# Three eighths of one streamed V unit held on chip, an eighth of it in the scores' PSUM bank; raw left rows by slot; streamed units at new places

## The chip, the cores and the metric

One core of one Trainium2 chip. The metric is the device time of one execution in microseconds (us), the median of several.

## The reference

Two branches on the layer-normed rows of x (2048 rows of 1024), added to x:

```python
x = A_x
xn = _layernorm(x, axis=-1)
return x + _A_ref(xn, ...) + _B_ref(xn, ...)      # B: gelu(xn @ w1 + b1) @ w2 + b2, F = 3584
...
for s in range(64):                                # A: 64 segments of 32 rows, 8 memory rows ahead of each
    h = concatenate([mem, xs])
    q, k, v = h @ Wq, h @ Wk, h @ Wv               # each 1024 x 4096: 32 heads of 128
    p = softmax(mask(q k^T / sqrt(128)))
    o = (p v) @ Wo                                 # 4096 x 1024
    mem = o[:8]                                    # goes into the next segment
    outs.append(o[8:])
```

The memory rows make the segments a chain. Wq, Wk, Wv and Wo are 8 MB each in bf16, 32 MB together, and are multiplied anew in every segment; they don't fit on chip.

## The kernel before

The program first computes branch B (to about 400 us of the profile), and then runs the loop over the 64 segments.

**Units.** The four weights are cut into 64 units of 128x2048 bf16 (512 KB): (w, i, u) is row block i and half u of the columns for K, Q and V; an O unit is two heads. `ORDER` takes them pass by pass: K0, Q0, K1, Q1, V0, V1 of eight units each, then 16 O units. 47 units are resident in SBUF. The other 17 are streamed: `PLACED` holds four strings of passes, one for each type of segment (s mod 4), where "S" is a place for a streamed unit and "." for a resident one. The first string also says which units are streamed.

**Streams.** Six SBUF slots take the streamed units in turn. `unit_done` follows the last product of a streamed unit and calls `start_stream`, which starts the next unit into the slot just freed: a DMA on SP's queue from a packed DRAM copy (`Wc_...`), 128 rows of 4096 B. So a start runs six streamed units ahead of its use. Two of the 17 units are not fetched: `IN_PSUM` and `IN_BANKS` are kept in two PSUM banks each, and `copy_bits` (L274, DVE) copies them into the slot; `late_by` starts them `LATER` = 4 places later.

**Left rows.** The last 8 of a segment's 32 rows don't depend on the memory. Those of four segments (a group) are multiplied as one set of 32 rows, `hL`, as extra "left" products beside the 24 + 8 rows of the segment: K0 and K1 in type 0, V0 in type 1, Q0 and V1 in type 2, Q1 in type 3; O in type 3 takes them with a wider accumulator. `hL` is renewed for the next group in three pieces: slots 0 and 1 after K1 of type 0, slot 2 after Q0 of type 2, slot 3 after Q1 of type 3 (`renew_left`, by DVE in the first seven segments, then by POOL). The raw rows lie in a tile of their own, `left_rows_in` (128x256), loaded once a group (L297) before O of type 3. `VL[u]` (128x512) holds the left values by slot, 128 columns each; `by_slot` writes all of VL[0] at the start of type 2 and all of VL[1] at the start of type 3, and a segment reads the columns of its own slot.

**A segment.** Six passes of products (L831), with the attention of the first half of the heads placed into K1, Q1 and V1, that of the second half into V1 and O. The tables `SCORES_0`, `SUMS_0`, `ATTEND`, `VALUES_0`, `SUMS_1` and `VALUES_1` say after which unit of a pass each step comes, by type. Scores, sums and the memory's transpose (`put_mem`) use one PSUM bank, `mixed`:

```python
mixed = banks.tile([P, 512], F32, name="mixed", ...)   # 0:224 scores, 0:320 sums, 224:288 put_mem, 468:512 masks
```

O's products (L1068) end in `fold` (types 0 to 2), whose result goes through `put_mem` into the next segment's rows. While DVE does that, PE computes up to six left products of the next segment's pass ahead (`lead_products`). Every engine runs its instructions in the order in which they are written here.

Of the kernel before, what the change touches and what calls it, by code (L numbers as in the profile page):

```python
# [10 lines left out]
BF16 = mybir.dt.bfloat16  # L11
U32 = mybir.dt.uint32
# [5 lines left out]
P = 128  # L18
S = 2048
# [5 lines left out]
SEG = 32  # L25
MEM = 8
NSEG = S // SEG
KT = DM // P
# [9 lines left out]
NX = 24  # L38
NL = SEG - NX
GRP = 4  # L40
# [14 lines left out]
MEM_AT = 20  # L55
EARLY_SEGS = 7
LEAD_FIRST = 4
SCORES_0 = (6, 6, 6, 6)
SUMS_0 = (4, 4, 4, 4)
ATTEND = (0, 0, 1, 0)  # L60
VALUES_0 = ((4, 4), (4, 4), (3, 5), (4, 4))
SUMS_1 = (6, 6, 5, 7)
VALUES_1 = (5, 5, 5, 5)
LATER = 4
LAG = 3
STREAM_BUFS = 6
# [7 lines left out]
def pass_order():  # L74
# [12 lines left out]

ORDER = pass_order()
PLACED = (
    "..SS...." ".S..S..." "S....S.." "S......S" "S......." "S.S...S." "...SS..." "S....S.S",  # L90
    ".S.S...." "S....S.." ".S.S...." "....S..S" "......S." "SS...S.." "....S.S." "S....SS.",
    "..SS...." ".S..S..." "S...S..." "....S.S." "..S....." "...S.S.S" "...S..S." "S....SS.",
    "...SS..." ".S..S..." "..S..S.." ".SS....." "..S....." "S...S..S" "...S..S." "S....S.S",
)
IS_STREAMED = {unit: PLACED[0][n] == "S" for n, unit in enumerate(ORDER)}
assert all(placed.count("S") == STREAMED for placed in PLACED)
# [13 lines left out]
RESIDENT = [unit for unit in ORDER if not IS_STREAMED[unit]]  # L110

IN_PSUM = [unit for unit in ORDER if IS_STREAMED[unit]][3]
STREAMED_O = [unit for unit in ORDER[48:] if IS_STREAMED[unit]]

IN_BANKS = STREAMED_O[AT_BANKS]
# [5 lines left out]
def kernel(  # L121
# [16 lines left out]
    nc = tc.nc  # L138
# [38 lines left out]
    slabs = ctx.enter_context(tc.tile_pool(name="slabs", bufs=1))  # L177
    consts = ctx.enter_context(tc.tile_pool(name="consts", bufs=1))
    hrp = ctx.enter_context(tc.tile_pool(name="hrp", bufs=1))
    left_rows_in = hrp.tile([P, 256], BF16, name="left_rows_in")  # L180
    hL = hrp.tile([P, 256], BF16, name="hrL").rearrange("p (k t) -> p k t", k=KT)
    ctx.enter_context(tc.manual_schedule())

# [52 lines left out]
    for k in range(7):  # L236
# [4 lines left out]
    res_tiles = {}  # L241


    copies = {
        unit: dram.tile([P, 2048], BF16, name="Wc_" + "_".join(map(str, unit)))[:, :]
        for unit in reversed(ORDER) if IS_STREAMED[unit] and unit not in KEPT
    }

    def fetch(t, unit):
        w, i, u = unit  # L250
        if w == "O":
            h = 4 * i + 2 * u
            nc.sync.dma_start(out=t.rearrange("p (h d) -> p h d", d=DM), in_=Wo_v[:, h:h + 2, :])
        else:
            nc.sync.dma_start(out=t, in_=W_v[w][:, i, 2048 * u:2048 * u + 2048])

    def fetch_resident(*places):
        for place in places:
# [13 lines left out]
    def copy_bits(out, in_):  # L272

        nc.vector.tensor_single_scalar(out=out, in_=in_, scalar=0, op=ALU.bitwise_or)  # L274

    def start_stream(slot):
        if not starts:
            return
        n = starts.popleft()
        unit, t = streams[n], slab(slot)  # L280
        if unit in kept_in:
            for c0, bank in kept_in[unit]:
                copy_bits(t[:, c0:c0 + 1024].bitcast(U32), bank.bitcast(U32))
        elif unit in copies:
            nc.sync.dma_start(out=t[:, :], in_=copies[unit])
        else:
            fetch(t[:, :], unit)
        stream_tiles[n], slot_of[n] = t, slot

    nxt, kept_in = {}, {}  # L290

    def load_x_rows(s, eng=nc.sync):
        eng.dma_start(out=homes[s % 2], in_=rows_d[s, :, :])
        nxt["hT"] = homes[s % 2].rearrange("p (k t) -> p k t", k=KT)

    def load_left_rows(g, out, eng=nc.sync):
        eng.dma_start(out=out, in_=rowsL_d[g, :, :])  # L297

    def renew_left(rows, s0, s1, eng):

        eng.tensor_copy(
            out=hL.rearrange("p k (t s) -> p k t s", s=GRP)[:, :, :, s0:s1],
            in_=rows.rearrange("p (k s t) -> p k t s", k=KT, s=GRP)[:, :, :, s0:s1],
        )

    sp = ctx.enter_context(tc.tile_pool(name="sp", bufs=1))
# [50 lines left out]
    with tc.tile_pool(name="ma", bufs=2) as ma:  # L357
# [112 lines left out]
                    )  # L470

        def keep_xT(tg, xnT):
            xl = [t[:, 0:512].rearrange("p (g k i t) -> p g k i t", g=2, k=KT, i=GRP) for t in ko_flat]
            for half in range(2):
                nc.sync.dma_start(
                    out=rows_d[16 * tg:16 * tg + 16, :, 128 * half:128 * half + 128].rearrange("s p c -> p s c"),
                    in_=xnT[half].rearrange("p s k t -> p s (k t)"),
                )
                for g in range(4):
                    nc.gpsimd.tensor_copy(  # L480
                        out=xl[g // 2][:, g % 2, 4 * half:4 * half + 4, :, :],
                        in_=xnT[half][:, 4 * g:4 * g + 4, :, NX:SEG].rearrange("p i k t -> p k i t"),
                    )
            for k in range(2):
                nc.sync.dma_start(
                    out=rowsL_d[4 * tg + 2 * k:4 * tg + 2 * k + 2, :, :].rearrange("g p c -> p g c"),
                    in_=xl[k][:, :, :, :, :].rearrange("p g k i t -> p g (k i t)"),
                )

        def keep_R(ttg, rsb):  # L490
# [92 lines left out]
        for tg in range(4):  # L583
            last = tg == 3
            if last:

                load_x_rows(0)
                load_left_rows(0, pd_main[:, 0:256])
                load_left_rows(1, left_rows_in[:, :])
# [146 lines left out]
    with tc.tile_pool(name="late", bufs=1) as late:  # L736
# [60 lines left out]

        hT = nxt["hT"]
        VL = [late.tile([P, 512], BF16, name=f"VL{u}") for u in range(2)]
        led = {}  # L800

        for s in range(NSEG):
# [16 lines left out]
            mover = nc.vector if s < EARLY_SEGS else nc.gpsimd  # L819
            st = {}  # L820

            def product(w, i, t, lhs, acc, seq, left=False):
                for j in range(4):
                    o, m = acc[32 * j:32 * j + 32, :], t[:, 512 * j:512 * j + 512]
                    if w != "V":
                        o = o.rearrange("p (h e) -> p h e", e=32)
                        m = t.rearrange("p (h q e) -> p q h e", q=4, e=32)[:, j, :, :]
                    elif left:
                        o = o.rearrange("p (q c e) -> p q c e", q=4, e=32)
                        m = m.rearrange("p (c q e) -> p q c e", q=4, e=32)  # L830
                    nc.tensor.matmul(  # L831
                        o,
                        lhsT=lhs[:, i, :],
                        rhs=m,
                        start=(i == seq[0]),
                        stop=(i == seq[-1]),
                        tile_position=(0, 32 * j),
                    )

            def lead_products(n):  # L840

                w, u, psL, ahead, order = led["next"]
                for _ in range(n):
                    if led["made"] < len(ahead):
                        i = ahead[led["made"]]
                        product(w, i, res_tiles[w, i, u], hL, psL, order, True)
                        led["made"] += 1

            def half_pass(w, u, left, at, left_done=None):
# [13 lines left out]
                for n in range(KT + lag):  # L863
                    if n < KT:
                        tiles[now[n]] = unit_tile((w, now[n], u))
                        product(w, now[n], tiles[now[n]], hT, ps, now)
                    if n < lag:
                        continue
                    i = now[n - lag]
                    t = tiles.pop(i)  # L870
                    if left and i not in ahead:
                        product(w, i, t, hL, psL, order, True)
# [216 lines left out]
            if first:  # L1089
                keep(IN_BANKS, 1024, d_oL[:, 0:DM], 2)  # L1090
                keep(IN_BANKS, 0, kq[:, 0:DM], 3)
                copy_bits(mixed[:, 468:512].bitcast(U32), mask.bitcast(U32))
            psK, psKL = half_pass(
                "K", 0, left_k[0], {0: [lambda: by_slot(i4 - 2, qL_flat[i4 - 2])]} if i4 >= 2 else {},
                lambda ps: turn_kL(ps, 0),
# [8 lines left out]
            psQ, psQL = half_pass("Q", 0, left_q[0], {} if left_q[0] else {1: [lambda: q_left(0)]}, first_queries)  # L1104
            turn_q(psQ)
            if i4 == 2 and more:
                renew_left(left_rows_in, 2, 3, mover)
            psK1, psK1L = half_pass("K", 1, left_k[1], {SCORES_0[i4]: [lambda: scores(0)]})
            if i4 == 0 and not first and more:
                renew_left(left_rows_in, 0, 2, mover)  # L1110
            exps(0)
            st["kT", 1] = nat_home
            rows_out(psK1, nat_home, nc.scalar.copy)
# [8 lines left out]
                q_left(1)  # L1122
            turn_q(psQ1)
            if i4 == 3 and more:
                renew_left(left_rows_in, 3, 4, mover)
            if not final and not first:
                load_x_rows(s + 1, loads)

# [26 lines left out]
                staged(1)(psV1L)  # L1155
            if first:
                by_slot(1, hr_home)
                renew_left(left_rows_in, 0, 2, mover)
                load_x_rows(s + 1, loads)
            loads.dma_start(out=homes[s % 2], in_=res_d[s + 1, :, :])  # L1160
            if i4 == 3 and g + 2 < NGRP:
                load_left_rows(g + 2, left_rows_in[:, :])
            at = {VALUES_1[i4]: [lambda: values(1, (0, 1))]}
            psX = new_acc()
            for n, unit in enumerate(O_UNITS):
# [5 lines left out]
                unit_done(unit)  # L1171
                for fn in at.get(n, ()):
                    fn()
                if n == 6 and left_o:
                    st["resL"] = pd_main[:, 0:256]
                    loads.dma_start(
                        out=st["resL"], in_=resL_d[g, :, :]
                    )
# [97 lines left out]
```

## Time and profile before

| | us |
|---|---|
| median of 3 runs | 1772.6 |
| lowest, highest | 1770.92, 1780.19 |
| profiled execution | 1783.28 |
| its span, first to last instruction | 1781.5 |

| engine | busy in the span |
|---|---|
| PE (products) | 1694.8 us, 95% |
| DVE | 1019.5 us, 57% |
| ACT | 696.5 us, 39% |
| POOL | 287.2 us, 16% |

The profile shows the core's engines (PE, its weight loads PEld, DVE, ACT, POOL, and SP, which only issues DMAs here) and 16 DMA engines, which all queues share. "SPq" is SP's queue of DMA issues. In a row of instructions, "x48" is a count, and the brackets hold the engine's idle time before it and who ended it. A row of waits has the total in us, the number of waits and the longest. "DMA share" is the mean busy share of the 16 DMA engines. The granted clock of PE was 0.996.

### The profile page before, as it was taken

To read this page: it belongs to the slowest core of one execution; us is meant where nothing else is said; L and a number is where in the kernel's file an instruction comes from. 1 tells how busy PE (TensorE), PEld (TensorE's weight loads), DVE (VectorE), ACT (ScalarE), POOL (GpSimd) and SP (SyncE) were. 2 spreads that over 40 slices of the span, in tenths; PEclk is the share of its full clock that TensorE was granted. 3 is DMA by queue.
4 is the path that set the end of the run, shared out by engine and by line. 5 is a ranking of instruction groups with operands and counts; after the bars stand their busy time and mean duration, and the time that the engine had idled before them with its cause. 6 is when DMAs were issued, how large, how long until landed. Compare 5 with 4: busy or idle time off the path is not lost.

```text
span 1781.5 us, 65947 instructions
## 1 busy us (share of the span) xinstructions
PE 1694.8 (95%) x28354; PEld 838.9 (47%) x28374; DVE 1019.5 (57%) x2592; ACT 696.5 (39%) x1743; POOL 287.2 (16%) x575
## 2 busy tenths in 40 slices
PE   9999999998998999999999999999999999999998
PEld 5444444444444444444444444444444444444444
DVE  7657483825555565655655555555565656565564
ACT  6334251602333444433344333443333444343333
POOL 0000002403120211111211111121111121111120
PEclk9999999999999999999999999999999999999999
DMA  9455312779999999999999999999999999999997
GB/s 283 141 171 167 98 36 66 272 270 322 387 379 364 384 387 383 399 377 395 384 384 387 376 378 384 394 369 388 382 400 377 398 378 393 387 401 372 393 385 295
DMA packets 232072, 591.85 MB, mean 332 GB/s; under 512 B 57523, under 2 KB 88051, under 8 KB 231780
## 3 DMA queue, kind: packets, MB, share of 16 engines
q1 hardware_dynamic: 199680, 568.05, 84.7%
q0 software_dynamic: 15680, 14.35, 2.5%
q10 hardware_dynamic: 16420, 5.25, 1.2%
q8 instruction: 222, 3.64, 0.8%
q14 instruction: 70, 0.57, 0.1%
HBM read 571.50 MB, written 26.74 MB: 336 GB/s over the span
## 4 chain that ended last, share of the span: by engine, by line
PE 41%; DMA 20%; DVE 5%; ACT 3%; issue 1%; DVEq 0%; SPq 0%; ACTq 0%
PE acc L831 27%; PE acc L1068 11%; DMA u<-Wc_O 8%; DMA u<-Wc_Q 5%; DMA u<-Wc_V 3%; DMA u<-Wc_K 2%; PE acc L1018 1%; DVE kq L919 1%; DMA hr_home<-res_d 1%; ACT mixed L991 1%; ACT qL L885 1%; PE mixed L944 1%; DVE pd_main L999 1%; PE mixed L328 1%; PE acc L1024 0%
## 5 line engine op out<-in xcount | busy, mean ns | idle before, releaser
L831 PE MATMUL acc<-u,hr_home 128*32 128x512 bf16 x11520 | 758.1, 381 | 37.1 <-DMA u<-Wc_V 19.7
L831 PEld LDWEIGHTS <-hr_home 128*32 128x32 bf16 x12288 | 333.0, 97 | 336.7 <-issue 58.4
L831 PE MATMUL acc<-u,hrL 128*32 128x512 bf16 x3008 | 258.8, 381 | 0.5 <-issue 0.5
L532 PE MATMUL ps<-u 128*128 128x512 bf16 (+1 forms) x992 | 195.0, 359 | 0.0
L885 ACT CAST d_oL<-acc 128x512 bf16<-128x512 f32 x143 | 83.0, 583 | 245.0 <-PE acc L831 226.5
L274 DVE TENSOR_SCALAR u<-kept 128x512 uint32<-128x512 uint32 x254 | 162.2, 679 | 27.8 <-PE acc L831 24.3
L1068 PE MATMUL acc<-u,d_oL 128*32 128x512 bf16 x2560 | 164.8, 382 | 6.8 <-DMA u<-Wc_O 5.8
L662 PE MATMUL ps<-u 128*128 128x512 bf16 x657 | 145.2, 379 | 0.8
L1068 PE MATMUL acc<-u,kq 128*32 128x256 bf16 (+1 forms) x2688 | 133.3, 321 | 10.6 <-DMA u<-Wc_O 7.7
L532 PEld LDWEIGHTS <-u 128*128 128x128 bf16 x992 | 91.6, 98 | 101.6
L999 DVE TENSOR_TENSOR pd_main<-kq,mixed 128x320 bf16<-128x320 bf16 x128 | 62.5, 488 | 126.9 <-ACT mixed L991 126.9
L1068 PEld LDWEIGHTS <-kq 128*32 128x32 bf16 x3328 | 87.5, 97 | 87.4 <-ACT kq L1037 26.7
L915 ACT CAST kq<-acc 128x256 bf16<-128x256 f32 x256 | 89.3, 375 | 96.4 <-PE acc L831 56.6
L1238 POOL DMA_DIRECT2D out_dram<-hr_home x168 | 85.0, 513 | 250.3 <-DVE hr_home L1208 250.1
L968 DVE TENSOR_TENSOR kq<-kq,mixed 128x96 bf16<-128x96 bf16 x128 | 26.2, 205 | 169.2 <-ACT kq L961 91.2
L919 DVE STREAM_TRANSPOSE kq<-kq 128x256 bf16<-128x256 bf16 x256 | 98.1, 421 | 28.0 <-ACT kq L915 28.0
L831 PEld LDWEIGHTS <-hrL 128*32 128x32 bf16 x3200 | 84.8, 97 | 54.9 <-issue 4.9
L889 ACT CAST kq<-acc 128x512 bf16<-128x512 f32 x128 | 75.2, 587 | 74.4 <-PE mixed L950 72.0
L662 PEld LDWEIGHTS <-u 128*128 128x128 bf16 x672 | 65.6, 98 | 78.7 <-DVE u L619 0.4
L611 ACT ACTIVATE u<-ps,b1col 128x512 bf16<-128x512 f32 x112 | 76.5, 684 | 65.4 <-PE ps L532 62.5
L991 ACT ACTIVATE mixed<-mixed,small_consts 128x160 f32<-128x160 f32 x256 | 94.2, 368 | 8.4
L1068 PEld LDWEIGHTS <-d_oL 128*32 128x32 bf16 x2560 | 62.9, 97 | 62.3 <-issue 12.3
(137 smaller groups left out, 1851.4 us busy)
## 6 DMA issues: line engine op xcount, KB each, us to landing
u<-Wc_K SPq DMA_DIRECT2D x256, 512.0 KB
u<-Wc_V SPq DMA_DIRECT2D x256, 512.0 KB
u<-Wc_O SPq DMA_DIRECT2D x256, 512.0 KB
u<-Wc_Q SPq DMA_DIRECT2D x192, 512.0 KB
u<-in_B_w_dram SPq DMA_DIRECT2D x28, 512.0 KB
u<-in_A_Wq_dram SPq DMA_DIRECT2D x13, 512.0 KB
u<-in_A_Wv_dram SPq DMA_DIRECT2D x12, 512.0 KB
u<-in_A_Wk_dram SPq DMA_DIRECT2D x9, 512.0 KB
```

What stands on the lines that cost most here:

```text
L274: nc.vector.tensor_single_scalar(out=out, in_=in_, scalar=0, op=ALU.bitwise_or)
L532: nc.tensor.matmul(ps[:, SEG * s0:SEG * s1].rearrange("p (s t) -> p s t", t=SEG), lhsT=w1_sb[fb // 2][:, kt, (fb % 2) * P:(fb % 2 + 1) * P ...
L611: nc.scalar.activation(out=xb[:, :], in_=ps[:, :], func=ACT.Identity, bias=b1col[:, fb:fb + 1], scale=1.0)
L662: nc.tensor.matmul(ps[:, :], lhsT=gts[fc // 4][:, fc % 4, t * P:(t + 1) * P], rhs=w2_sb[fc // 2][:, fc % 2, cs], start=(fc == 0), stop=(fc ...
L831: nc.tensor.matmul(o, lhsT=lhs[:, i, :], rhs=m, start=(i == seq[0]), stop=(i == seq[-1]), tile_position=(0, 32 * j),)
L885: cp(out=out, in_=ps.rearrange("p (h e) -> p h e", e=32))
L915: nc.scalar.copy(out=q_home[:, h0:h1, NL:40], in_=ps[:, 32 * h0:32 * h1].rearrange("p (h e) -> p h e", e=32))
L919: nc.vector.transpose(out=half, in_=half)
L991: nc.scalar.activation(out=mixed[:, 160 * b:160 * b + 160], in_=mixed[:, 0:160], func=ACT.Exp, scale=-1.0, bias=off[:, b:b + 1],)
L999: nc.vector.tensor_tensor(out=pdA.rearrange("p c b q -> p b c q"), in0=prA[:, None, :, :].to_broadcast([P, 2, 4, 40]), in1=dd, op=ALU.mult,)
L1068: nc.tensor.matmul(acc[r0:r0 + rows, 0:256 * len(blocks)], lhsT=lhsT, skip_group_check=True, rhs=o_columns(t, k, blocks), start=start, sto ...
L1238: loads.dma_start(out=out_flat[rows, 256 * j:256 * j + 256], in_=res[32 * j:32 * j + NX, :])
```

## The change

**Three eighths of unit V (0, 1) stay on chip.** Only its first 1280 of 2048 columns are streamed (`COMING`). Columns 1536 to 2048 lie in a new SBUF tile `part`, from which the fourth product reads. Columns 1280 to 1536 (128x128 words of 32 bits) are kept in `mixed`, at columns 320 to 448; `start_stream` copies them with DVE into the slot beside each DMA. Both are loaded once, ahead of segment 0, the eighth by way of VL[0].

**Raw left rows by slot.** `left_rows_in` goes. The rows lie in DRAM by slot now, and are loaded in three pieces a group: slot 2 before O of type 1 into VL[1]'s columns 0 to 64, slot 3 before O of type 2 into VL[0]'s columns 256 to 320, slots 0 and 1 before O of type 3 into VL[0]'s columns 256 to 384: columns that no segment reads at that time. In segment 0 slots 0 and 1 come through `pd_main`, after O's seventh unit.

**New points.** 17 of the 32 pass strings of `PLACED` are new, the number of streamed units in each pass stays; the set of streamed units changes with the first string. Four steps move: scores(0) of type 2 one unit later, sums(0) of type 3 two earlier, sums(1) and values(1) of type 3 one earlier each.

```diff
-SCORES_0 = (6, 6, 6, 6)
-SUMS_0 = (4, 4, 4, 4)
+SCORES_0 = (6, 6, 7, 6)
+SUMS_0 = (4, 4, 4, 2)
...
-SUMS_1 = (6, 6, 5, 7)
-VALUES_1 = (5, 5, 5, 5)
+SUMS_1 = (6, 6, 5, 6)
+VALUES_1 = (5, 5, 5, 4)
...
 PLACED = (
-    "..SS...." ".S..S..." "S....S.." "S......S" "S......." "S.S...S." "...SS..." "S....S.S",
-    ".S.S...." "S....S.." ".S.S...." "....S..S" "......S." "SS...S.." "....S.S." "S....SS.",
-    "..SS...." ".S..S..." "S...S..." "....S.S." "..S....." "...S.S.S" "...S..S." "S....SS.",
-    "...SS..." ".S..S..." "..S..S.." ".SS....." "..S....." "S...S..S" "...S..S." "S....S.S",
+    "S..S...." "S...S..." "S...S..." "S....S.." "S......." "SS....S." "....SS.." "S....S.S",
+    ".S.S...." "S....S.." ".S...S.." "...S...S" "......S." "SS...S.." "....S.S." "S....SS.",
+    "..SS...." ".S.S...." "S....S.." "....S..S" ".......S" ".S...S.S" "...S..S." "S....SS.",
+    "...SS..." ".S..S..." "..S..S.." "..S....S" ".....S.." ".S..S..S" "...S..S." ".S...S.S",
 )
...
+PARTIAL = ("V", 0, 1)
+STAYS = 1536
+COMING = 1280
...
-    left_rows_in = hrp.tile([P, 256], BF16, name="left_rows_in")
...
+    def columns_of(unit):
+        return COMING if unit == PARTIAL else 2048
+
     copies = {
-        unit: dram.tile([P, 2048], BF16, ...
+        unit: dram.tile([P, columns_of(unit)], BF16, ...
...
         elif unit in copies:
-            nc.sync.dma_start(out=t[:, :], in_=copies[unit])
+            nc.sync.dma_start(out=t[:, 0:columns_of(unit)], in_=copies[unit])
+            if unit == PARTIAL:
+                copy_bits(t[:, COMING:STAYS].bitcast(U32), eighth[0].bitcast(U32))
...
-    def load_left_rows(g, out, eng=nc.sync):
-        eng.dma_start(out=out, in_=rowsL_d[g, :, :])
+    def load_left_rows(g, s0, s1, out):
+        nc.sync.dma_start(out=out, in_=rowsL_d[g, :, 64 * s0:64 * s1])
...
         VL = [late.tile([P, 512], BF16, name=f"VL{u}") for u in range(2)]
+        part = late.tile([P, 2048 - STAYS], BF16, name="part")
+        w, i, u = PARTIAL
+        nc.sync.dma_start(out=part[:, :], in_=W_v[w][:, i, 2048 * u + STAYS:2048 * u + 2048])
+        nc.sync.dma_start(out=VL[0][:, 0:256], in_=W_v[w][:, i, 2048 * u + COMING:2048 * u + STAYS])
+        raw_2, raw_3, raw_01 = VL[1][:, 0:64], VL[0][:, 256:320], VL[0][:, 256:384]
...
                 for j in range(4):
-                    o, m = acc[32 * j:32 * j + 32, :], t[:, 512 * j:512 * j + 512]
+                    o = acc[32 * j:32 * j + 32, :]
+                    m = part[:, :] if (w, i, u) == PARTIAL and j == 3 else t[:, 512 * j:512 * j + 512]
...
                 copy_bits(mixed[:, 468:512].bitcast(U32), mask.bitcast(U32))
+                eighth.append(mixed[:, 320:448])
+                copy_bits(eighth[0].bitcast(U32), VL[0][:, 0:256].bitcast(U32))
...
             loads.dma_start(out=homes[s % 2], in_=res_d[s + 1, :, :])
+            if i4 == 1 and more:
+                load_left_rows(g + 1, 2, 3, raw_2)
+            if i4 == 2 and more:
+                load_left_rows(g + 1, 3, 4, raw_3)
             if i4 == 3 and g + 2 < NGRP:
-                load_left_rows(g + 2, left_rows_in[:, :])
+                load_left_rows(g + 2, 0, 2, raw_01)
...
+                if n == 6 and first:
+                    load_left_rows(1, 0, 2, pd_main[:, 0:128])
+                    renew_left(pd_main[:, 0:128], 0, 2, mover)
```

More of the change, by code (lines that the diff above doesn't have):

```diff
@@ L112 @@
 IN_PSUM = [unit for unit in ORDER if IS_STREAMED[unit]][3]
+PARTIAL = ("V", 0, 1)
+STAYS = 1536
+COMING = 1280
+assert IS_STREAMED[PARTIAL]
 STREAMED_O = [unit for unit in ORDER[48:] if IS_STREAMED[unit]]
@@ L241 @@
     res_tiles = {}
+    def columns_of(unit):
+        return COMING if unit == PARTIAL else 2048
     copies = {
-        unit: dram.tile([P, 2048], BF16, name="Wc_" + "_".join(map(str, unit)))[:, :]
+        unit: dram.tile([P, columns_of(unit)], BF16, name="Wc_" + "_".join(map(str, unit)))[:, :]
         for unit in reversed(ORDER) if IS_STREAMED[unit] and unit not in KEPT
@@ L254, in fetch @@
         else:
-            nc.sync.dma_start(out=t, in_=W_v[w][:, i, 2048 * u:2048 * u + 2048])
+            nc.sync.dma_start(out=t, in_=W_v[w][:, i, 2048 * u:2048 * u + columns_of(unit)])
     def fetch_resident(*places):
@@ L288, in start_stream @@
         stream_tiles[n], slot_of[n] = t, slot
-    nxt, kept_in = {}, {}
+    nxt, kept_in, eighth = {}, {}, []
     def load_x_rows(s, eng=nc.sync):
@@ L302, in renew_left @@
             out=hL.rearrange("p k (t s) -> p k t s", s=GRP)[:, :, :, s0:s1],
-            in_=rows.rearrange("p (k s t) -> p k t s", k=KT, s=GRP)[:, :, :, s0:s1],
+            in_=rows.rearrange("p (s k t) -> p k t s", k=KT, s=s1 - s0),
         )
@@ L472, in keep_xT @@
         def keep_xT(tg, xnT):
-            xl = [t[:, 0:512].rearrange("p (g k i t) -> p g k i t", g=2, k=KT, i=GRP) for t in ko_flat]
+            xl = [t[:, 0:512].rearrange("p (g i k t) -> p g i k t", g=2, k=KT, i=GRP) for t in ko_flat]
             for half in range(2):
@@ L480, in keep_xT @@
                     nc.gpsimd.tensor_copy(
-                        out=xl[g // 2][:, g % 2, 4 * half:4 * half + 4, :, :],
-                        in_=xnT[half][:, 4 * g:4 * g + 4, :, NX:SEG].rearrange("p i k t -> p k i t"),
+                        out=xl[g // 2][:, g % 2, :, 4 * half:4 * half + 4, :],
+                        in_=xnT[half][:, 4 * g:4 * g + 4, :, NX:SEG],
                     )
@@ L486, in keep_xT @@
                     out=rowsL_d[4 * tg + 2 * k:4 * tg + 2 * k + 2, :, :].rearrange("g p c -> p g c"),
-                    in_=xl[k][:, :, :, :, :].rearrange("p g k i t -> p g (k i t)"),
+                    in_=xl[k][:, :, :, :, :].rearrange("p g i k t -> p g (i k t)"),
                 )
@@ L587 @@
                 load_x_rows(0)
-                load_left_rows(0, pd_main[:, 0:256])
-                load_left_rows(1, left_rows_in[:, :])
+                load_left_rows(0, 0, GRP, pd_main[:, 0:256])
                 renew_left(pd_main[:, 0:256], 0, GRP, nc.gpsimd)
@@ L820, with product @@
             st = {}
-            def product(w, i, t, lhs, acc, seq, left=False):
+            def product(w, i, u, t, lhs, acc, seq, left=False):
                 for j in range(4):
-                    o, m = acc[32 * j:32 * j + 32, :], t[:, 512 * j:512 * j + 512]
+                    o = acc[32 * j:32 * j + 32, :]
+                    m = part[:, :] if (w, i, u) == PARTIAL and j == 3 else t[:, 512 * j:512 * j + 512]
                     if w != "V":
@@ L845, in lead_products @@
                         i = ahead[led["made"]]
-                        product(w, i, res_tiles[w, i, u], hL, psL, order, True)
+                        product(w, i, u, res_tiles[w, i, u], hL, psL, order, True)
                         led["made"] += 1
@@ L865, in half_pass @@
                         tiles[now[n]] = unit_tile((w, now[n], u))
-                        product(w, now[n], tiles[now[n]], hT, ps, now)
+                        product(w, now[n], u, tiles[now[n]], hT, ps, now)
                     if n < lag:
@@ L871, in half_pass @@
                     if left and i not in ahead:
-                        product(w, i, t, hL, psL, order, True)
+                        product(w, i, u, t, hL, psL, order, True)
                     if first and (w, i, u) == IN_PSUM:
@@ L1106 @@
             if i4 == 2 and more:
-                renew_left(left_rows_in, 2, 3, mover)
+                renew_left(raw_2, 2, 3, mover)
             psK1, psK1L = half_pass("K", 1, left_k[1], {SCORES_0[i4]: [lambda: scores(0)]})
             if i4 == 0 and not first and more:
-                renew_left(left_rows_in, 0, 2, mover)
+                renew_left(raw_01, 0, 2, mover)
             exps(0)
@@ L1124 @@
             if i4 == 3 and more:
-                renew_left(left_rows_in, 3, 4, mover)
+                renew_left(raw_3, 3, 4, mover)
             if not final and not first:
@@ L1157 @@
                 by_slot(1, hr_home)
-                renew_left(left_rows_in, 0, 2, mover)
                 load_x_rows(s + 1, loads)
             loads.dma_start(out=homes[s % 2], in_=res_d[s + 1, :, :])
+            if i4 == 1 and more:
+                load_left_rows(g + 1, 2, 3, raw_2)
+            if i4 == 2 and more:
+                load_left_rows(g + 1, 3, 4, raw_3)
             if i4 == 3 and g + 2 < NGRP:
-                load_left_rows(g + 2, left_rows_in[:, :])
+                load_left_rows(g + 2, 0, 2, raw_01)
             at = {VALUES_1[i4]: [lambda: values(1, (0, 1))]}
```

## The prediction

> **What bounds the kernel now.** I read the page first: the engines, the slices, the DMA queues.
>
> ```profile
> span 1781.5 us, 65947 instructions
> PE 1694.8 (95%) x28354; PEld 838.9 (47%) x28374; DVE 1019.5 (57%) x2592; ACT 696.5 (39%) x1743; POOL 287.2 (16%) x575
> DMA  9455312779999999999999999999999999999997
> GB/s 283 141 171 167 98 36 66 272 270 322 387 379 364 384 387 383 399 377 395 384 384 387 376 378 384 394 369 388 382 400 377 398 378 393 387 401 372 393 385 295
> q1 hardware_dynamic: 199680, 568.05, 84.7%
> q0 software_dynamic: 15680, 14.35, 2.5%
> q10 hardware_dynamic: 16420, 5.25, 1.2%
> ```
>
> Two resources are near full in the loop over segments: PE (95%) and the 16 DMA engines ("9" in every slice from the tenth to the last but one). To tell which ends last I cut one group of four segments (types 0 to 3, with 16, 8, 16 and 8 extra left products and the wide O in the last) out by its ends, then asked what PE waits for, in all and in the group's third segment.
>
> ```profile
> L338 DVE CAST hr_home<-mixed x63: 224/225/226, 440.1 to 1753.9; 128x64 bf16<-128x64 f32 x63
> 1355.24:1376.41 21.17, 19.95 (x418) 9.79 (x418) 12.24 (x32) 8.77 (x24) 4.73 (x9) 1.00 0.97 357
> 1376.41:1396.40 19.99, 18.59 (x386) 9.32 (x386) 11.51 (x30) 7.70 (x22) 3.13 (x6) 1.00 1.02 400
> 1396.40:1416.90 20.50, 20.15 (x418) 10.53 (x418) 12.78 (x33) 8.76 (x24) 3.49 (x7) 1.00 1.02 398
> 1416.90:1439.50 22.60, 21.54 (x436) 10.68 (x435) 11.40 (x30) 8.51 (x23) 4.02 (x8) 1.00 1.02 393
> sum 84.26, PE 80.23 PEld 40.33 DVE 47.92 ACT 33.74 POOL 15.37; mean PE 20.06 PEld 10.08 DVE 11.98 ACT 8.43 POOL 3.84
> ```
>
> ```profile
> PE acc L831 <- DMA u<-Wc_V: 18.6, 25, 2.3
> PE acc L1068 <- DMA u<-Wc_O: 12.9, 29, 1.0
> PE acc L831 <- DMA u<-Wc_Q: 10.9, 18, 1.3
> PE mixed L944 <- DVE kq L919: 2.9, 19, 0.2
> PE acc L831 <- DVE u L274: 2.8, 6, 1.1
> ```
>
> The L338 row has one cast a segment: 62 periods from 440.1 to 1753.9 us, 21.19 us each, or 15.5 groups. In the windows (columns: length, PE, PEld, DVE, ACT, POOL, clock, DMA share, GB/s) the share is 1.02 in three types and 0.97 in type 0. The waits are those of 400 to 1700 us, 61.3 segments: 18.6 + 12.9 + 10.9 = 42.4 us behind streamed units, 0.69 us a segment and 2.8 a group, so PE alone would need about 84.3 - 2.8 = 81.5 us a group where 84.3 are spent. The transfers are the bound, and PE follows 3% behind. In type 2 PE is busy 20.15 of 20.50 us: that type is PE's own.
>
> **Part by part.** *The streamed bytes.* The page's queues price a packet: q1 took 84.7% x 16 x 1781.5 us / 199680 = 120.9 ns for a mean of 2845 B; q10 1.2% = 20.8 ns for 320 B. The line through both is 8.1 ns + 0.0396 ns/B, and q0 (2.5%, 45.4 ns at 915 B) lies within 1.1 ns of it. A unit is 128 rows of 4096 B, 8 an engine: 8 x 170.5 = 1.364 us. V (0, 1) at 1280 columns has rows of 2560 B: 8 x 109.6 = 0.877 us. Saved: 0.487 us a segment, 1.95 a group. Through q0 and q1 alone the slope is 0.0391 and the saving 1.92; by bytes at the windows' 393 GB/s, 196.6 KB are 0.50 us, 2.0 a group.
>
> *Raw left rows by slot.* Before, one load a group of 128 rows of 512 B; after, three, of 256, 128 and 128 B: 8 x (18.3 + 13.2 + 13.2) - 8 x 28.4 = +0.13 us a group. They go through SP behind the V units' starts, as the one load did.
>
> ```profile
> 908.88 6.63 DMA u<-Wc_Q
> L297 SPq DMA_DIRECT2D left_rows_in<-rowsL_d x15: 319/427/1560, 313.7 to 1599.6; - x15
> L301 POOL COPY hrL<-left_rows_in x40: 299/324/331, 579.0 to 1678.1; 128x64 bf16<-128x64 bf16 x27, 128x128 bf16<-128x128 bf16 x13
> ```
>
> A transfer takes 6.6 us from issue to landing in a full queue (the chain's row). Slot 2's rows are issued before O of type 1 and wanted by POOL after Q0 of type 2, some 32 units later; at 0.23 us a unit (below) that is 7.4 us without the attention between: they land in time. The renewals stay three a group, of the same sizes, 0.3 us on POOL. SP pays 0.43 us for each of two more issues; ahead of a streamed unit's start that is 0.9 us a group on a queue that mostly waits for slots, and I cost it at nothing: the cover is the four or five transfers in flight.
>
> The Trainium skill, "DMA: Bandwidth & Descriptors", Specifications, gives 512 B as the least transfer for full line rate and says that less is read, modified and written. If that doubles the new rows, as an estimate, a group pays 0.36 us more. No row here shows rows of 128 B alone.
>
> *The eighth.* One DVE copy of 128x128 uint32 out of PSUM a segment.
>
> ```profile
> L274 DVE TENSOR_SCALAR u<-kept x254: 651/681/693, 433.7 to 1767.4; 128x512 uint32<-128x512 uint32 x127
> 404.55 0.20 DVE L274 TENSOR_SCALAR mixed<-qL 128x44 uint32<-128x44 uint32 x1
> 907.21 0.21 PE L328 MATMUL mixed<-ident_mem,kq 128*128 128x32 bf16 x2
> 910.12 1.25 DVE L274 TENSOR_SCALAR u<-kept 128x512 uint32<-128x512 uint32 x2
> 913.80 0.28 PE L944 MATMUL mixed<-kq,d_oL 128*32 128x40 bf16 x16
> 914.20 0.36 ACT L964 ACTIVATE kq<-mixed 128x224 bf16<-128x224 f32 x1 [1.03 <-PE mixed L950]
> 914.71 0.18 DVE L969 TENSOR_TENSOR kq<-kq,mixed 128x64 bf16<-128x64 bf16 x1
> 916.51 2.78 PE L831 MATMUL acc<-u,hr_home 128*32 128x512 bf16 x48
> 917.12 0.56 POOL L293 DMA_DIRECT2D hr_home<-rows_d  x1 [0.48 <-issue]
> ```
>
> Between 44 columns (0.20 us) and 512 (0.68) lies 0.28 us for 128. Starts run six slots ahead and the two units kept in PSUM later, so this one comes when the segment's fourth streamed unit, Q0's second, is done. Behind it in DVE's order stand Q0's transposes, and scores(0) comes only after K1's seventh or eighth unit, at 0.23 us a unit 1.6 us or more after Q0. DVE is busy 48 of 84 us. Cost: nothing; without that cover 0.28 us a segment. The bank it reads, `mixed`, lies idle between put_mem (907.21) and the scores (913.80), which is where Q0 stands.
>
> *New points.* The count of streamed units a pass doesn't change, only their places. A unit is 4 products, 2.78 us / 12 = 0.23 us, so a move by one place is 0.23 us against a backlog of five transfers of 1.36 us: while the transfers are the bound it changes where PE waits, not how much. Two places can hurt. In type 2 Q0's second, copied from PSUM by DVE, is wanted one unit earlier, where PE already waits for L274 now and then: 0 to 0.23 us a group. In type 3 sums(0) comes after Q1's third unit instead of its fifth; from the first score (913.80) to the masked exponentials (914.89) are 1.09 us, and PE has 0.35 (scores) + 4 x 0.23 + one left product ahead: 1.5 us. No wait.
>
> *Segment 0.* `part` and VL's eighth (196.6 KB) are loaded once more, 0.49 us. DVE's copy of the eighth to PSUM now waits for that load, and the casts of the left keys, which free a bank for PE, stand behind it.
>
> ```profile
> 395.72 6.51 SPq L253 DMA_DIRECT2D u<-in_A_Wo_dram  x4
> 404.93 0.69 DVE L885 CAST d_oL<-acc 128x512 bf16<-128x512 f32 x1 [0.19 <-PE acc L831]
> 420.00:425.00 5.00, 2.41 (x44) 0.97 (x40) 2.11 (x3) 0.00 (x0) 2.19 (x4) 1.00 1.03 409
> ```
>
> SP can issue it at about 402 us, behind the last four resident units; with two of those ahead it lands near 407, and DVE's casts of the left keys, at 404.93 before, come some 2 us late. At 420 to 425 PE is busy 2.41 of 5 us at 409 GB/s, so most of that is hidden. At the end of the segment DVE waits for the slots' rows (O's seventh unit) ahead of the fold. Together -1 to +6 us; I take +2.
>
> *Sum.* At most 1.95 - 0.13 = 1.82 us a group. PE's room is 2.8, so a group could come to 82.4 us against PE's 81.5. Not all of it will be had: in type 2 PE sets the time, and what is saved there must be carried by six slots into type 3; in type 0 the engines already idle a little (0.97). I take 1.5 a group, between 0.84 (types 1 and 3 alone, 2 x 0.487 - 0.13) and 1.82: 15.5 x 1.5 = 23.3, less 2: 21 us. The profiled execution took 1783.28 us, 1.78 more than its span, and would come to 1762; the median of the runs is 1772.6, 10.7 below it, and from there it is **1751 us**. With the ends: 1772.6 - 28.2 - 1 = 1743 and 1772.6 - 13 + 6 = 1766.
>
> **The rivals.** *PE becomes the bound in types 0 and 2.* For it: type 2's 0.35 us outside PE's work. The gain is then 0.84 a group, 13 us less 2: 1762. Against: 0.9 us of type 0's time in this group is a wait for O's transfer.
>
> *The eighth gets on the path.* Where DVE is late, its 0.28 us stand ahead of the scores: 63 x 0.28 = 18 us, and 21 - 18 leaves 1770. The L944 row says PE does wait for the queries' transpose, 19 times for 2.9 us, but in the second half's scores, not here. The Trainium skill, "PSUM — Partial Sum Buffer", PSUM bank collisions raise a hardware error, wants two engines kept apart by bank and quadrant, not by address, so the scores would have to wait for this read. The rows above show the bank idle then.
>
> *Slower: a burst of V and O units.* Type 2 now asks for V0's last place, then V1's second, sixth and last: four streamed units in nine places, where before the same four stood over fourteen. If the slots are empty there, PE waits as in the longest V wait, 2.3 us a group; 1.5 - 2.3 = -0.8, 15.5 groups: 12 us lost and 2 at the start, 1787. It decides from 1.5 us a group on. Against: while queues never run dry, a wait at one place is taken off another.
>
> *Slower: VL is guarded whole.* Slot 2's load goes into VL[1] just before values(1) of type 1 reads another part of it, six units of 0.23 us later; PE would wait 6.6 - 1.4 = 5.2 us, 15 times: 1751 + 78 = 1829. Against: at 917.12 POOL loads one half of `hr_home` while PE reads the other without a wait.
>
> *It doesn't do what it says:* packets cost by number, not bytes. The line of three queues speaks against; it would give 1772.6 + 2 + 2 = 1777.
>
> **How the numbers follow.** The forecast has 0.62, PE's bound 0.16, the eighth on the path 0.06, packets by number 0.03, the burst 0.09, VL whole 0.04. A measurement of this kernel can tell 0.5% (8.9 us) from no change. Faster by more: the forecast, and 0.14 of PE's bound (its 1762 lies just inside): 0.76. Within: 0.02 + 0.06 + 0.03 = 0.11. Slower: 0.13. The range runs from 1736, which is 7 us under that end of 1743 (a sixth of PE's 42 us of waits for units, in case the new places take some away), to 1770: outside lie the slower cases, packets by number and 0.02 below.
>
> **What would show it.** Right: q1 has 11 MB to 13 MB less; L274 shows 128x128 copies at 0.28 us; the windows of types 1 and 3 are 0.4 to 0.7 us shorter, type 2 stays at 20.5; PE's waits for V, O and Q fall from 42 to about 20 us. Wrong: DMA share still 1.0 with the same group length (bytes were not the price), waits of L944 for DVE (the eighth), of L1024 for a DMA (VL), or of L831 for Wc_V above 18.6 us (the burst).

## The result, and the profile after

| | us |
|---|---|
| changed kernel, median of 5 runs | 1754.39 (1752.37 to 1756.29) |
| kernel before, median of 5 runs | 1772.57 |
| ratio, 95% interval | 0.9894 [0.987, 0.9919] |
| profiled execution of the changed kernel | 1756.29 |

18 us were gained where 21 were forecast. The number came out; the reason given for it did not, and most of this text is about that.

The page of the changed kernel, the same lines as before:

```profile
span 1754.6 us, 66199 instructions
PE 1686.8 (96%) x28354; PEld 836.2 (48%) x28374; DVE 1034.0 (59%) x2657; ACT 694.9 (40%) x1743; POOL 288.4 (16%) x575
...
DMA  9455311878999999999999999999999999999997
GB/s 281 150 161 177 101 35 49 273 262 307 371 384 366 372 388 376 391 384 398 379 383 377 393 384 384 390 372 397 369 396 381 391 382 392 378 398 367 391 380 297
...
q1 hardware_dynamic: 204288, 555.46, 84.6%
```

q1 moved 12.6 MB less, as forecast, but the DMA row still shows nines and GB/s is what it was (384 before, 383 after, from 500 to 1700 us): fewer bytes in less time. One group of segments (types 0 to 3; length, PE, PEld, DVE, ACT, POOL, clock, DMA share, GB/s), and PE's waits from 400 to 1700 us:

```profile
1335.07:1355.63 20.56, 19.86 (x418) 9.80 (x417) 12.42 (x33) 8.78 (x24) 4.75 (x9) 1.00 0.96 360
1355.63:1375.62 19.99, 18.68 (x386) 9.38 (x385) 11.91 (x31) 7.70 (x22) 3.14 (x6) 1.00 1.03 401
1375.62:1396.14 20.52, 20.08 (x418) 10.44 (x418) 13.08 (x34) 8.77 (x24) 3.51 (x7) 1.00 1.01 386
1396.14:1417.77 21.63, 21.25 (x436) 10.80 (x434) 11.53 (x31) 8.38 (x23) 4.03 (x8) 1.00 1.02 394
```

```profile
PE acc L1082 <- DMA u<-Wc_O: 9.0, 21, 1.0
PE acc L845 <- DMA u<-Wc_V: 8.1, 18, 1.1
...
PE acc L845 <- DVE d_oL L899: 6.4, 1, 6.4
PE acc L845 <- DMA u<-Wc_Q: 3.5, 9, 1.1
```

The group is 1.6 us shorter: type 3 lost 1.0, type 0 0.6, types 1 and 2 nothing. PE's waits for units fell from 42 to 21 us. What is new is a single wait of 6.4 us for DVE, in segment 0.

Below, "group" is the mean length of each type's segments, cut at the memory's cast (L338 in the kernel before), over the 50 segments from 13 to 62 (the first is 0), added up over the four types. In brackets are PE's waits for units, by type.

| kernel | type 0 | type 1 | type 2 | type 3 | group |
|---|---|---|---|---|---|
| before | 20.98 (0.57) | 20.05 (1.16) | 20.88 (0.17) | 22.60 (0.71) | 84.51 |
| before, profiled again | 20.70 (0.34) | 20.18 (1.42) | 20.75 (0.15) | 22.50 (0.61) | 84.13 |
| changed | 20.64 (0.06) | 19.84 (1.18) | 20.43 (0.00) | 21.82 (0.10) | 82.73 |

Each row is a single execution. The two of the kernel before are 0.38 us a group apart, and other profiled executions lay from 4.6 us below to 8.0 us above the median of their kernel. So a few tenths of a microsecond a group prove nothing alone; times are compared by their medians.

### The profile page after: what moved, and what is told of

The parts are those of the page before. It is cut to its first block, busy times and chain, and to the rows that moved or that the text cites. A ratio compares the mean times of both kernels' runs of the same rounds, so it can differ in the third digit from the quotient of the medians.

```text
span 1754.6 us, 66199 instructions
## 1 busy us (share of the span) xinstructions
PE 1686.8 (96%) x28354; PEld 836.2 (48%) x28374; DVE 1034.0 (59%) x2657; ACT 694.9 (40%) x1743; POOL 288.4 (16%) x575
## 5 line engine op out<-in xcount | busy, mean ns | idle before, releaser
L845 PE MATMUL acc<-u,hr_home 128*32 128x512 bf16 x11456 | 757.9, 380 | 15.1 <-DMA u<-Wc_V 8.1
L845 PEld LDWEIGHTS <-hr_home 128*32 128x32 bf16 x12288 | 332.8, 97 | 308.5 <-issue 34.2
L845 PE MATMUL acc<-u,hrL 128*32 128x512 bf16 x2991 | 259.2, 382 | 9.0 <-DVE d_oL L899 6.4
L281 DVE TENSOR_SCALAR u<-kept 128x512 uint32<-128x512 uint32 x254 | 162.1, 679 | 33.0 <-PE acc L845 23.2
L845 PEld LDWEIGHTS <-hrL 128*32 128x32 bf16 x3200 | 85.0, 97 | 64.9 <-issue 16.1
```

The source lines that it names most:

```text
L845: nc.tensor.matmul(o, lhsT=lhs[:, i, :], rhs=m, start=(i == seq[0]), stop=(i == seq[-1]), tile_position=(0, 32 * j),)
```

## The experiments

Theory at first: the transfers are the bound, and the bytes kept on chip are the gain. Rivals: the places and moved steps are the gain; PE is the bound already. The first four runs take the parts apart. Ratios are to the kernel before, run beside them on the same chip.

**The whole unit streamed again.** From the changed kernel:

```diff
-COMING = 1280
+COMING = 2048
-        part = late.tile(...)            # and both loads ahead of segment 0, and the eighth's copies
-                    m = part[:, :] if (w, i, u) == PARTIAL and j == 3 else t[:, 512 * j:512 * j + 512]
+                    m = t[:, 512 * j:512 * j + 512]
```

> The changed kernel with the whole of V (0, 1) streamed again (no part, no eighth); new places, moved steps and raw rows by slot stay. Theory (bytes are the price, places change nothing while the transfers are the bound): the group of four segments is back at 84.3 us from 82.7, time 1770 to 1776, and PE's waits for units back at some 40 us. Rival 1 (the new places and moved steps brought the gain): 1752 to 1757. Rival 2 (each brought about half): near 1763.

Measured: 1757.44 us, 0.9896 [0.9877, 0.9915], group 82.99. This is close to rival 1: with every byte back the gain is still there. The bytes aren't worth nothing, though: segment 0 is 5.3 us shorter here than in the changed kernel (below), so the rest of the loop is some 5 us longer by the medians. The window from 500 to 1700 us and its waits, after those of the kernel before:

```profile
PE acc L831 <- DMA u<-Wc_V: 13.2, 21, 2.3
PE acc L1068 <- DMA u<-Wc_O: 11.7, 26, 1.0
PE acc L831 <- DMA u<-Wc_Q: 10.1, 16, 1.3
```

```profile
500.00:1700.00 1200.00, 1153.80 (x23714) 585.24 (x23704) 691.72 (x1781) 486.58 (x1347) 219.80 (x427) 1.00 1.02 393
PE acc L839 <- DMA u<-Wc_V: 10.6, 21, 0.8
PE acc L1076 <- DMA u<-Wc_O: 7.7, 20, 0.8
PE acc L839 <- DMA u<-Wc_Q: 2.9, 5, 1.3
```

The same bytes through the same six slots move at 393 GB/s, where the kernel before (window below) has 384, and the waits fall from 35.0 to 21.2 us.

**The old places.** The changed kernel with `PLACED`, `SCORES_0`, `SUMS_0`, `SUMS_1` and `VALUES_1` of before; three eighths stay on chip.

> The changed kernel with the places and step tables of before; three eighths of V (0, 1) stay on chip. Theory (bytes): 1753 to 1758, a group of 82.5 to 83. Rival 1 (places): 1770 to 1775. Rival 2 (half each; the places are needed now that PE is near the bound): near 1763.

Measured: 1781.31 us, 1.0037 [1.0021, 1.0054], group 84.52. None of the three figures expected: 12.6 MB less, and slower than before. Windows of 500 to 1700 us, of the kernel before, then of this one, and its waits:

```profile
500.00:1700.00 1200.00, 1137.71 (x23236) 574.01 (x23232) 675.86 (x1736) 474.26 (x1308) 215.49 (x419) 1.00 1.00 384
```

```profile
500.00:1700.00 1200.00, 1138.89 (x23240) 574.59 (x23236) 688.60 (x1794) 474.52 (x1308) 215.48 (x419) 1.00 1.00 375
```

```profile
PE acc L1082 <- DMA u<-Wc_O: 15.7, 30, 1.5
PE acc L845 <- DMA u<-Wc_Q: 13.4, 25, 1.1
PE acc L845 <- DMA u<-Wc_V: 6.6, 12, 1.3
```

The rate went down with the bytes, from 384 to 375 GB/s, PE waits as long as before (35.7 us), and the DMA share is 1.00 both times. A share of 1.00 thus doesn't show saturation. The trace's packet records say why: the share adds up the packets' times, and these overlap. More than 16 packets are in flight 30% of the time in the kernel before and 28% here; in 15% and 19% of it there are fewer than 16, so that some engine has nothing to do. The group is as long as before; segment 0 takes 98.9 us, 1.7 and 4.3 more than in the two profiles of the kernel before (below), which is a good part of the 5 us lost.

**A quarter kept, not three eighths.** The changed kernel without the eighth:

```diff
-COMING = 1280
+COMING = 1536
-        nc.sync.dma_start(out=VL[0][:, 0:256], ...)       # and both kinds of the eighth's copies
```

> The changed kernel with 1536 columns of V (0, 1) streamed: part alone stays on chip, the eighth in the scores' bank goes with its copies. 0.326 of 0.487 us of transfers a segment are saved. Theory (bytes, in proportion): two thirds of 18 us, 1759 to 1762. Rival (PE is the bound already, so the last eighth brought nothing, or its copy cost as much as it saved): 1752 to 1756. Segment 0's wait of PE for the eighth (6.4 us) goes too: up to 2 us less in each case.

Measured: 1750.67 us, 0.9861 [0.9841, 0.9881], group 82.62. Fewer columns kept, and no slower: the proportion of the theory is gone. The group is that of the changed kernel (82.73); the median is lower because segment 0's wait goes too (92.9 us, not 98.9).

**Half of an O unit cut as well.**

```diff
-            nc.sync.dma_start(out=t[:, 0:columns_of(unit)], in_=copies[unit])
+            cut = 1024 if unit == STREAMED_O[0] else columns_of(unit)
+            nc.sync.dma_start(out=t[:, 0:cut], in_=copies[unit][:, 0:cut])
...
-                            rhs=o_columns(t, k, blocks),
+                            rhs=o_columns(t, 0 if unit == STREAMED_O[0] else k, blocks),
```

> The changed kernel with the first streamed O unit cut to half as well (1024 of 2048 columns; its second head is multiplied with the first head's columns, so that output is not the reference's). 8 x (170.5 - 89.2) = 0.65 us of transfers less a segment. If the transfers still were the bound everywhere: 41 us less, 1713. If PE is the bound in types 0, 2 and 3 and only type 1 waits (1.18 us a segment, 16 segments): at most 19 us less, 1735 to 1745, with almost no waits of PE for units left and DMA share below 1.

Measured: 1752.85 us, 0.9866 [0.9848, 0.9885], group 82.44. By the ratios that is 5 us less than the changed kernel, about a quarter of what even the PE theory allowed at most:

```profile
500.00:1700.00 1200.00, 1158.67 (x23846) 585.54 (x23842) 706.03 (x1844) 487.10 (x1349) 219.84 (x427) 1.00 1.00 373
```

373 GB/s at a share of 1.00 again, with fewer than 16 packets in flight 22% of the time. Bytes do count where PE waits: type 1's segments went from 19.84 to 19.19 us. But types 2 and 3 gave 0.4 us of that back (20.61 and 22.05).

In the kernel before, the chain of waits shows what kind of waits these are; columns are start, length and what:

```profile
1365.10 6.54 DMA u<-Wc_O
1374.90 6.45 DMA u<-Wc_K
1386.38 6.77 DMA u<-Wc_O
1418.32 6.07 DMA u<-Wc_Q
```

Each runs from a start's issue to the moment when PE goes on: 6.1 to 6.8 us in these four, 5.6 to 8.3 in all 46 such rows between 500 and 1700 us, half of them under 6.7. A start comes six streamed units ahead, when a slot falls free; where PE uses up six in less than that, it waits. That is the new theory: it is slots and places that set the time, rather than the count of bytes.

**The new places alone, and one row of them.** The kernel before with all of the new `PLACED`; then with its fourth row only:

```diff
-    "...SS..." ".S..S..." "..S..S.." ".SS....." "..S....." "S...S..S" "...S..S." "S....S.S",
+    "...SS..." ".S..S..." "..S..S.." "..S....S" ".....S.." ".S..S..S" "...S..S." ".S...S.S",
```

> The kernel before with the new places and nothing else: step tables, left rows and whole units as before. New theory (six slots and 6.7 us from a start's issue to its landing: PE waits where six streamed units in a row are used up in less; the places decide): 1753 to 1760, type 3's segment 21.9 us instead of 22.6, type 0's 20.7 instead of 21.0. Rival (the moved steps did it): 1768 to 1775.

Measured: 1761.73 us, 0.9928 [0.9911, 0.9946]; types 20.59, 19.90, 20.68, 22.04, group 83.21. This is just outside the new theory's range and far from the rival's. Again the rate rises at the same bytes and slots, from 384 to 391 GB/s:

```profile
500.00:1700.00 1200.00, 1148.11 (x23622) 581.33 (x23614) 686.30 (x1768) 482.85 (x1336) 219.44 (x425) 1.00 1.01 391
```

> The kernel before with the fourth row of places alone (type 3; Q1's two neighbours at its second and third unit go to its third and last, V0 and V1 move with it). New theory: type 3 loses its 0.7 us of waits and types 0 to 2 stay as they are: 11 us less, 1759 to 1764. Rival (the places work together, or any row alone only moves the wait on): 1768 to 1775, with the 0.7 us in type 0 or 1 instead.

Measured: 1768.12 us, 0.9965 [0.995, 0.9981]; types 20.78, 20.12, 20.67, 22.09, group 83.66. The time is the rival's, not the 11 us less of the new theory. Type 3 does lose its waits for units (0.71 to 0.12), without a rise in the other types, but it gives some back: its other idle time grows from 0.38 to 0.64 us. A wait of the run with all the new places, then the same wait in the whole-unit run, which has the moved steps and the raw rows by slot too:

```profile
PE mixed L944 <- DVE kq L919: 7.2, 21, 0.5
```

```profile
PE mixed L952 <- DVE kq L927: 2.0, 13, 0.2
```

With the units there in time, scores come before DVE has turned the queries. In the whole-unit run most of that wait is gone, and from 0.9928 to 0.9896 are 5.6 us, though the two intervals touch. Which of the four steps does it, or whether the raw rows have a part, wasn't tried.

**A seventh slot.** The kernel before, then the changed one:

```diff
-                fetch_resident("late0", "late1")
+                fetch_resident("late0")
+                res_tiles[UNIT_AT["late1"]] = res_tiles[UNIT_AT["late0"]]
+                start_stream("late1")
```

> The kernel before with a seventh slot. Its room comes from one resident unit, whose products read another resident unit's tile, so the output is not the reference's; places, bytes and number of products stay. New theory (starts come too late, the 16 engines have time to spare): a start comes one streamed unit, 1.4 us, earlier, most of the 42 us of waits for units go, 1732 to 1748, at the same bytes and over 395 GB/s in the loop. Theory on record (the transfers are the bound): 1770 to 1775, no change.

Measured: 1745.95 us, 0.9843 [0.9823, 0.9863]; types 20.55, 18.99, 20.70, 22.16, group 82.40.

```profile
500.00:1700.00 1200.00, 1157.81 (x23853) 585.43 (x23849) 692.98 (x1792) 489.15 (x1350) 221.77 (x431) 1.00 1.02 395
```

```profile
PE acc L1070 <- DMA u<-Wc_O: 6.9, 15, 0.8
PE acc L833 <- DMA u<-Wc_Q: 5.0, 10, 0.7
...
PE acc L833 <- DMA u<-Wc_V: 1.2, 3, 0.5
```

Old places, all the bytes, and 395 GB/s instead of 384; the waits for O, Q and V from 500 us on fall from 35.0 (11.7 + 10.1 + 13.2) to 13.1 us. This settles that the engines could move more than they did, if only 3%, and that earlier starts get it. Not all 27 us are the slot's: segment 0, with one resident unit less to load, takes 90.8 us, 4 to 6 less than before.

> The changed kernel with a seventh slot, its room taken as in the run on the kernel before (one resident unit's products read another's tile, so the output is not the reference's). New theory (late starts are all that is left to win): the waits left in type 1 (1.2 us a segment) mostly go, types 0, 2 and 3 stay at 20.6, 20.4 and 21.8: 10 to 18 us below the changed kernel, 1735 to 1745, and close to the kernel before with seven slots. Rival (the changed kernel is PE's already): 1750 to 1756.

Measured: 1736.82 us, 0.9781 [0.9759, 0.9803]; types 20.56, 18.52, 20.67, 21.62, group 81.37. Type 1's 1.18 us of waits are down to 0.09, and the other types stay within 0.25 us. In the changed kernel units hold PE up in one type, and there an earlier start removes the wait; in the other three types it changes next to nothing.

**Segment 0.** The changed kernel's 6.4 us wait, in DVE's timeline:

```profile
403.52 0.20 DVE L281 TENSOR_SCALAR mixed<-qL 128x44 uint32<-128x44 uint32 x1
410.10 0.29 DVE L281 TENSOR_SCALAR mixed<-VL 128x128 uint32<-128x128 uint32 x1 [6.38 <-DMA VL<-in_A_Wv_dram]
410.30 0.68 DVE L899 CAST d_oL<-acc 128x512 bf16<-128x512 f32 x1
```

```profile
405.00:410.00 5.00, 0.00 (x0) 0.00 (x0) 0.00 (x0) 0.21 (x1) 1.58 (x3) 0.80 1.02 373
410.00:415.00 5.00, 3.97 (x40) 1.68 (x43) 3.36 (x6) 0.32 (x2) 1.47 (x4) 0.52 1.04 401
```

DVE stands behind the eighth's load, the casts that free a bank stand behind it in DVE's order, and PE does nothing for the five us shown. When it goes on, its granted clock is 0.52 in the next five: the first eight units take 0.43 us each instead of 0.22, 1.7 us more on top of the wait. From the first rows' memory cast to the end of segment 0 are 98.9 us here, 93.6 with the whole unit, 97.2 and 94.6 in the two profiles of the kernel before. First the copy was moved behind K0's turn:

> The changed kernel with one move: in segment 0 DVE copies the eighth to its bank after K0's turn, no longer ahead of the casts of the left keys. If the 5 us that segment 0 lost come from PE waiting 6.4 us for those casts behind the load: 1748 to 1752. Rival (the loads of part and the eighth themselves delay the units behind them): 1753 to 1756.

Measured: 1752.29 us, 0.9876 [0.9856, 0.9896], segment 0 97.0 us. That lies between the two expectations. PE now waits 5.8 us, in two waits, for the casts of the left queries: one cast on, much the same wait. Then the load was moved ahead:

```diff
                 start_stream("xn2")
                 start_stream("xn3")
+                w, i, u = PARTIAL
+                nc.sync.dma_start(out=pd_main[:, 0:256], in_=W_v[w][:, i, 2048 * u + COMING:2048 * u + STAYS])
...
-        nc.sync.dma_start(out=VL[0][:, 0:256], in_=W_v[w][:, i, 2048 * u + COMING:2048 * u + STAYS])
...
-                copy_bits(eighth[0].bitcast(U32), VL[0][:, 0:256].bitcast(U32))
+                copy_bits(eighth[0].bitcast(U32), pd_main[:, 0:256].bitcast(U32))
```

> The changed kernel with the eighth loaded some 45 us earlier, into pd_main, so that DVE finds it there at the start of segment 0. If segment 0's loss is DVE standing behind that load: PE's 6.4 us of waits for casts in segment 0 go, the segment ends 4 to 6 us earlier, 1747 to 1751. Rival (the units behind are late anyway): 1752 to 1756.

Measured: 1749.32 us, 0.9857 [0.9829, 0.9884], segment 0 92.7 us: the 6 us are back. With the run that keeps a quarter (0.9861) and the next one (0.9859) it is the fastest whole computation here, though all three intervals touch that of the changed kernel. The last run moves places in type 1's row on top of this:

> As e11, and in type 1's row V0's unit one place earlier and the last O places at 2, 7 and 8 instead of 1, 6 and 7. New theory: type 1's waits, the only ones left, fall by some 0.2 us a segment, 3 us in all: 1744 to 1748. Rival (a wait only moves on): as e11.

Measured: 1748.30 us, 0.9859 [0.9836, 0.9882]. By the ratios there is no gain over the early load alone. In the trace type 1's waits fell from 1.09 to 0.81 us while types 2 and 3 are 0.1 and 0.3 us longer, but this profiled execution lay 8.0 us above the median, so the trace can't say why.

**The kernel before once more.**

> The kernel before, profiled once more, because its first profiled execution (1783.28 us) lay 10.7 us above its median while the others lie within 2 us of theirs. If that execution was a drawn-out one: this profile near 1773, a group of 83.8 to 84.1 us instead of 84.5, with the waits of types 0, 1 and 3 still there but smaller by some 8 us in all. Rival (profiling costs this kernel 10 us): near 1783 again, the same waits.

Measured: 1777.04 us, group 84.13; another execution beside it took 1778.33. The time lies between the two figures, so neither expectation is borne out. The first profiled execution was 6.2 us longer than this one, and the waits of types 0, 1 and 3 are nearly the same in both (2.44 and 2.37 us a group). The traces are 27 or 21 us from that of the changed kernel, where the medians are 18 apart.

## Why the prediction was right, and where its reason was wrong

**What bounds the kernel: wrong.** The step that failed is "The transfers are the bound", read from a DMA share of 1.02 beside PE's waits for DMAs. The share stayed between 1.00 and 1.02 from 373 GB/s (the cut O unit) to 395 (seven slots). PE's waits for units were real, but fewer bytes at the old places left them as they were (35.0 and 35.7 us), while the new places alone, at the same bytes, took them to 19.6 (11.7 for V, 7.1 for O, 0.8 for Q) and one more slot to 13.1: the units were started too late. Most of the signs of being right that the prediction named did come (12.6 MB less, copies of 0.28 us, waits from 42 to 21 us), but they can't tell the bytes from the places. What it put down as PE's own time, 81.5 us a group, was right: 81.37 with seven slots and hardly a wait for units.

**The streamed bytes: priced right, worth little.** A 2560 B packet took 107.9 ns on average, where 109.6 were taken. Saved transfer time was put at 1.95 us a group and 1.5 of it taken as gain, 23 us in all. With new places the step from the whole unit to three eighths is 82.99 to 82.73 in the traces, 0.26 us a group or 4 us; by the medians, with segment 0's wait out of the way, it is 6 to 7 us (0.9896 to 0.9861 with a quarter kept, to 0.9857 with the early load). With old places the group stays (84.51 or 84.13 to 84.52).

**Raw left rows: right.** In the trace's packet records a 128 B row took 13.0 ns and a 256 B row 18.2, as the line over the queues said (13.2 and 18.3). The Trainium skill's rule on rows under 512 B ("DMA: Bandwidth & Descriptors", Specifications), taken as a doubling, doesn't show here.

**The eighth: right inside the loop.** 64 copies of 0.28 us, and the scores don't wait for them (PE's six waits for L281, 2.1 us in all, are of L845):

```profile
L281 DVE TENSOR_SCALAR u<-mixed x64: 276/282/293, 415.1 to 1731.3; 128x128 uint32<-128x128 uint32 x64
```

**New points: wrong, and the cause of the gain.** That a move "changes where PE waits, not how much" followed from the first step. The places alone gave 12.8 us (0.9928); type 3's row alone gives 6.2. The moved steps, of which one was looked at ("No wait") and none was given a gain, brought 5.6 more together with the raw rows by slot. The forecast had types 1 and 3 shorter by 0.4 to 0.7 us and type 2 unchanged; by the means over the loop it was 0.7 or 0.8 in type 3, 0.2 or 0.3 in type 1, and 0.3 to 0.5 in type 2.

**Segment 0:** +2 us taken, 4.3 measured against the second profile of before (98.9 and 94.6), 1.7 against the first, inside -1 to +6. The wait at the start was put at 2 us and was 6.4; the load landed at 410 us, not 407. Loading the eighth earlier gave 6.2 us of it back.

So the sum closes otherwise than written: 12.8 + 5.6 = 18.4 us from places, steps and raw rows, 4 to 7 from the bytes, 4 to 6 lost in segment 0. That 21 was forecast and 18 came is luck: one term was far too large (23 us for the bytes) and another was put at nothing (the new points). Of the rivals, the burst of V and O units named the right mechanism, places against slots, with the wrong sign: waits for V fell from 18.6 to 8.1 us. PE's bound in types 0 and 2 was right as a state (20.6 to 20.8 and 20.4 to 20.7 us in every run with the new places or a seventh slot), wrong as what the change would do.

**Open:** what the 6.7 us of a landing consist of. With seven slots the chain's rows are longer, 8.1 us in the middle one of 27, so part of a landing is the queue of the transfers ahead of it, and in that the engines' rate still counts. A shorter landing with six slots wasn't tried. Which of the moved steps matter is open too.

## What to carry to other kernels

A DMA share of 1.00 doesn't show that the engines can do no more: look whether GB/s moves when bytes, places or buffers do, before bytes are priced as time. With a ring of n buffers, compare the time from issue to landing under load with the time in which the consumer uses up n pieces at the densest place. Where the second is shorter, moving pieces apart or adding a buffer can win more than fewer bytes; here it did. And a one-time load at a stage's start costs whatever stands in order behind the engine that waits for it, so load it before anybody needs it.

## What the runs showed of the hardware that was not expected

The mean busy share of the 16 DMA engines read 1.00 at 373, 375 and 384 GB/s and 1.02 at 395, while fewer than 16 packets were in flight 22%, 19%, 15% and 6% of the time. One more buffer raised the rate of the same transfers by 3% (384 to 395 GB/s), other places by 2% (384 to 391). And a landing got longer with more in flight: in the chain's rows from 500 to 1700 us 5.6 to 8.3 us with six slots, 4.9 to 10.1 with seven, of which this is the longest:

```profile
632.83 10.08 DMA u<-Wc_O
```
